# Loading k of batch 1 ahead of the weights, and moving batch 1's first attention steps ahead of batch 0's cosines

## The chip, the cores and the metric

The kernel runs on one core of a Trainium2 chip. The metric is the device time of one execution in microseconds (us). Lower is better. Each comparison was made on one chip, with the kernel before run in the same rounds. Nearly all executions fell in the normal ("fast") state, and only those are compared. The profiled execution gives the span, which is about 1.8 us shorter than the time.

## The reference

Two parts follow each other. An attention compresses k and v through 32 packed queries p, then attends from q to the result. A gated layer follows, with cos as the gate.

```python
# q, k, v: (8 batches, 8 heads, 576, 64), p: (8, 8, 32, 64), float32
p_packed = sm_attn(p, k, v)               # softmax(p k^T / 8) v
out      = sm_attn(q, p_packed, p_packed) # softmax(q p_packed^T / 8) p_packed
x = out.transpose(0, 2, 1, 3).reshape(8 * 576, 512)
h = x @ w_in                              # 512 -> 2048
y = (h * cos(h)) @ w_out                  # 2048 -> 512, written as float32 (4608, 512)
```

The kernel forms `PPW = p_packed @ w_in` for each batch, so that h of a batch comes straight from the normalised second softmax `a2n`.

## The kernel before

In the traces the instructions of each engine run in the order of the program (below, for one, SP holds a transpose back for 14 us behind another one). One stage per batch interleaves three things: the exps of batch s, then the 16 slices of its h (matmul on TensorE, cosine on ScalarE, multiply on VectorE), and "filler": the output matmuls of batch s-1, 16 for each of 4 or 5 chunks of rows. Three PSUM buffers (`psA`) serve everything but the output. Some names: `pe_T` transposes k or q on TensorE and `xbar` by DMA; `s1` is the scores and exps of p k^T, and `a1_pe` or `a1_xbar` transposes these exps (`a1`); `pp` forms the packed values and `ppw` one of the four pieces of PPW; `s2`, `sums2` and `normalise` are the second softmax; `dup_p` and `pack_p` prepare p; `warm` is matmuls on zeros whose result nobody reads; `gate` is a copy of one element, with which POOL waits for a tile. The parts that the change and the argument touch (cuts are marked `# ...`):

```python
def load(n, b):                       # k, v or q of a batch, float32 -> bf16, issued by POOL
    bf[n, b] = bf_pool.tile([TP, H, C * D], BF16, name=n + "bf", tag=n + "bf")   # one buffer each
    G.dma_start(out=bf[n, b], in_=...)

def xbar(n, b):                       # transpose by DMA, on the SP queue
    nc.sync.dma_start_transpose(out=xT[n, b], in_=bf[n, b]...)
def a1_xbar(b):                       # the same for a1, the exps of p k^T
    nc.sync.dma_start_transpose(out=a1T[b], in_=a1[b % 2]...)
def pp(b): ...                        # packed values: needs a1T and the permuted v

def out_gen(b):                       # one output matmul per next(); stores go out on the SP queue
    for c in range(n_chunks(b)):
        for fc in range(NFC): ...     # all of w_out for each chunk
        copy((V, ACT)[n_out[0] % 2], osb, ps)
        for a, z, rows in pieces_of(b, c):
            nc.sync.dma_start(out=rows, in_=osb[a:z, :])

# start: loads in the order k0 v0 q0, w_in (p in between), w_out, k1 v1 q1 k2 v2 q2
# ... attention of batch 0, then its h, then:
set_filler(0)
fill(4); pe_T("k", 1); fill(3); s1(1); permute_v(1, V); fill(8); a1_pe(1)   # ... 43 filler matmuls
# ... between the steps of batch 1's attention

def begin_loads(b):                   # POOL waits for the k transpose of b, then loads
    G.tensor_copy(out=gate, in_=xT["k", b][0:1, 0, 0:1])
    for n, i in (("v", b), ("q", b), ("k", b + 1)):
        load(n, i)

permute_v(2); xbar("q", 2); xbar("k", 3)          # ahead of the h of batch 1
slot(1, [...], [(8, lambda: begin_loads(3))])     # h of batch 1, loads hooked to slice 8

for s in range(2, B):
    # ...
    s2(s); fill(8)
    s1(s + 1)
    xbar("q", s + 1); xbar("k", s + 2); a1_xbar(s + 1)     # SP queue, in this order
    G.tensor_copy(out=gate, in_=a1T[s + 1][0:1, 0, 0, 0:1])  # later loads wait for a1T
    # ... sums, normalise, fill, loads of s + 2, then
    slot(s, [(5, lambda: pp(s + 1)), ...], [])
```

The softmax here doesn't subtract the row's maximum and nothing guards it: scores larger than these inputs give would overflow.

## Time and profile before

| | before |
|---|---|
| time, median of the first 3 runs | 266.17 us (263.6 to 266.24) |
| span of the profiled execution | 262.1 us |
| TensorE (PE) busy | 241.2 us, 92% |
| first cosine of batch 0 / last multiply of its h ends | 21.1 / 38.0 us |
| cosine table load ahead of the h of batch 1 / 2 / 3 / 7 | 56.4 / 82.9 / 112.9 / 224.5 us |

The last row is used as a set of markers: ScalarE loads a table when it changes between exps and cosines, and each stage has one such load ahead of its h. In the page, the first line below is the busy time of the engines. The other one is the TensorE clock that was granted, in tenths of full speed, for 40 equal slices of the span.

```profile
...
PE 241.2 (92%) x2003; PEld 132.1 (50%) x2037; DVE 158.7 (61%) x247; ACT 172.4 (66%) x276; POOL 53.8 (21%) x67
...
PEclk9997999999999999999999999999999999999999
...
```

Where TensorE idles is in the windows view of the kernel before (per window: its length, then busy time and count for each engine, granted clock, DMA share, GB/s):

```profile
...
0.00:20.00 20.00, 15.07 (x154) 8.04 (x157) 8.84 (x25) 8.79 (x16) 10.54 (x19) 1.00 1.06 175
20.00:40.00 20.00, 14.57 (x118) 8.62 (x119) 15.05 (x22) 14.03 (x20) 2.49 (x3) 0.91 1.26 206
40.00:80.00 40.00, 36.61 (x401) 20.57 (x406) 27.10 (x46) 26.72 (x48) 13.28 (x14) 1.00 1.09 177
80.00:240.00 160.00, 157.03 (x1241) 85.42 (x1262) 103.94 (x151) 120.67 (x191) 26.84 (x31) 1.00 0.70 130
...
```

Most of the idle time is in the first 80 us (13.8 us; another 4 are in the tail); from 80 to 240 us TensorE is busy 98% of the time. From 10 to 60 us the DMA engines are full as well (share above 1): k0, v0, q0, w_in, w_out, k1, v1, q1 and then batch 2's k, v and q land one after the other. The transposes of k1 on TensorE wait for that queue (timeline of the kernel before, TensorE):

```profile
...
39.01 1.15 PE L101 MATMUL psA<-ident,kbf 96*128 96x96 bf16 x23 [1.65 <-DMA kbf<-in_k_dram]
```

The bracket says that it was idle for 1.65 us and that the load of k1 ended it.

POOL passes its gate on k3 and issues the loads of v3, q3 and k4 from 68.1 us on (timeline of the kernel before, POOL), and TensorE waits for that a1 transpose only 0.3 us (waits view: us in total, times, longest):

```profile
...
68.01 0.18 POOL L410 COPY gate<-kT 1x1 bf16<-1x1 bf16 x1
...
68.90 0.77 POOL L83 DMA_DIRECT2D qbf<-in_q_dram  x1
...
```

```profile
...
PE psA L162 <- DMA a1T<-a: 0.3, 1, 0.3
...
```

### The profile page before, as it was taken

The page shows a single profiled execution, that of the slowest core. Times are in us where ns is not written, and L with a number is a line of the kernel's source. Part 1 is how long each engine was busy: PE and PEld are TensorE (multiplying, and loading weights), DVE is VectorE, ACT ScalarE, POOL GpSimd, SP SyncE. Part 2 cuts the span into 40 slices and gives each one's busy share as a digit, 9 for nine tenths or more (in the row PEclk, how much of TensorE's full clock was granted, in tenths as well). Part 3 has the DMA queues.
Part 4 walks back from the last instruction along what each step waited for, and adds up shares of the span by engine and source line. Part 5 has one row for each costly group of instructions (what it writes and reads, how often), then busy time and mean ns, then how long its engine had stood idle before and what let it go on. Part 6 is the DMA issues. An engine that isn't in the chain of part 4 may idle for free.

```text
span 262.1 us, 5030 instructions
## 1 busy us (share of the span) xinstructions
PE 241.2 (92%) x2003; PEld 132.1 (50%) x2037; DVE 158.7 (61%) x247; ACT 172.4 (66%) x276; POOL 53.8 (21%) x67
## 2 busy tenths in 40 slices
PE   8777769899989999999999999999999999999993
PEld 3433436555545555456545654564446544565452
DVE  2457876749854797268836684378735873678110
ACT  1377762496698657987797668866796568875000
POOL 8523002440431220504050303120040000000000
PEclk9997999999999999999999999999999999999999
DMA  6999999999399899499959992899193111121232
GB/s 94 203 226 207 206 204 197 200 193 199 48 203 203 184 175 177 89 188 174 220 107 189 165 225 64 149 186 173 52 165 106 40 43 40 42 50 31 80 83 80
DMA packets 62919, 37.09 MB, mean 142 GB/s; under 512 B 35520, under 2 KB 58304, under 8 KB 62896
## 3 DMA queue, kind: packets, MB, share of 16 engines
q0 software_dynamic: 23168, 18.81, 47.2%
q1 hardware_dynamic: 39568, 17.83, 31.3%
q8 instruction: 16, 0.26, 0.4%
q10 hardware_dynamic: 160, 0.13, 0.2%
q14 instruction: 7, 0.06, 0.1%
HBM read 37.22 MB, written 9.44 MB: 178 GB/s over the span
## 4 chain that ended last, share of the span: by engine, by line
PE 68%; DMA 14%; ACT 7%; DVE 5%; issue 2%; POOL 1%; SPq 0%; DVEq 0%; ACTq 0%; POOLq 0%
PE ot L270 40%; PE psA L220 18%; DMA kbf<-in_k_dram 7%; DMA w_in_bf<-in_moe_w_in_dram 5%; PE psA L181 3%; DVE gT L227 2%; PE psA L162 2%; DMA a1T<-a 1%; ACT L423 1%; PE psA L123 1%; ACT cosT L224 1%; PE ot L259 1%; ACT PPW L74 1%; PE psA L197 1%; PE psA L101 1%
## 5 line engine op out<-in xcount | busy, mean ns | idle before, releaser
L270 PE MATMUL ot<-w_out_bf,gT 128*128 128x512 bf16 x483 | 126.1, 380 | 2.1 <-issue 1.1
L227 DVE TENSOR_TENSOR gT<-psA,cosT 128x576 bf16<-128x576 f32 x128 | 95.0, 755 | 31.9 <-ACT cosT L224 29.2
L224 ACT ACTIVATE cosT<-psA 128x576 bf16<-128x576 f32 x128 | 83.2, 653 | 40.7 <-PE psA L220 38.4
L220 PE MATMUL psA<-a2n,PPW 128*128 128x288 bf16 x512 | 84.5, 289 | 6.5 <-DVE gT L227 3.0
L220 PEld LDWEIGHTS <-PPW 128*128 128x128 bf16 x512 | 50.4, 98 | 43.8 <-issue 12.8
L270 PEld LDWEIGHTS <-gT 128*128 128x128 bf16 x512 | 47.0, 98 | 42.8 <-issue 7.3
L231 POOL COPY joint<-gT 128x512 bf16<-128x512 bf16 x16 | 9.8, 614 | 109.2 <-DVE gT L227 109.2
L207 DVE SCALAR_TENSOR_TENSOR a2n<-a2u,r,lns 128x576 bf16<-128x576 bf16 x16 | 12.4, 815 | 17.8 <-ACT lns L205 17.8
L76 DVE COPY osb<-ot 128x512 f32<-128x512 f32 (+1 forms) x19 | 12.7, 671 | 15.1 <-PE ot L270 12.1
L76 DVE CAST PPW<-psA 128x1024 bf16<-128x1024 f32 x16 | 19.5, 1221 | 2.0 <-PE psA L181 1.9
L74 ACT COPY osb<-ot 128x512 f32<-128x512 f32 (+1 forms) x18 | 10.4, 575 | 15.2 <-PE ot L270 10.4
L74 ACT CAST PPW<-psA 128x1024 bf16<-128x1024 f32 x16 | 16.1, 1009 | 1.1 <-PE psA L181 1.1
L76 POOL COPY vp<-vbf 96x3072 bf16<-96x3072 bf16 x6 | 16.5, 2749 | 1.4 <-DMA vbf<-in_v_dram 1.4
L181 PE MATMUL psA<-w_in_bf,ppT 64*32 64x512 bf16 x256 | 13.3, 392 | 0.1
L189 ACT ACTIVATE a2u<-psA,rs 128x576 bf16<-128x576 f32 x16 | 11.0, 738 | 2.5 <-PE psA L123 2.4
L132 ACT ACTIVATE a<-psA 128x576 bf16<-128x576 f32 x16 | 10.3, 651 | 3.4 <-PE psA L123 3.4
L270 PE MATMUL ot<-w_out_bf,joint 128*128 128x512 bf16 x45 | 12.2, 380 | 0.2
L199 ACT ACTIVATE lns<-psA 128x576 f32<-128x576 f32 x16 | 10.5, 658 | 2.4 <-PE psA L197 2.4
L172 ACT CAST ppT<-psA 64x128 bf16<-64x128 f32 x16 | 4.2, 261 | 11.5 <-PE psA L101 6.4
L141 DVE RECIPROCAL r<-sums 128x2 f32<-128x2 f32 x8 | 1.3, 161 | 16.7 <-ACT a L132 16.7
L83 POOL DMA_DIRECT2D kbf<-in_k_dram x8 | 6.3, 789 | 21.0 <-PE psA L101 17.1
L224 ACT ACT_TABLE_LOAD x8 | 10.3, 1283 | 0.1
(54 smaller groups left out, 149.7 us busy)
## 6 DMA issues: line engine op xcount, KB each, us to landing
kbf<-in_k_dram POOLq DMA_DIRECT2D x8, 576.0 KB, 11.3
vbf<-in_v_dram POOLq DMA_DIRECT2D x8, 576.0 KB, 6.3
qbf<-in_q_dram POOLq DMA_DIRECT2D x8, 576.0 KB, 9.6
out_dram<-osb SPq DMA_DIRECT2D x24, 192.0 KB, 2.9
out_dram<-osb SPq DMA_DIRECT2D x22, 128.0 KB, 2.4
w_in_bf<-in_moe_w_in_dram POOLq DMA_DIRECT2D x4, 512.0 KB, 15.4
w_out_bf<-in_moe_w_out_dram POOLq DMA_DIRECT2D x4, 512.0 KB, 20.0
out_dram<-osb SPq DMA_DIRECT2D x26, 64.0 KB, 2.2
```

What stands on the lines that cost most here:

```text
L74: ACT.copy(out=out, in_=in_)
L76: eng.tensor_copy(out=out, in_=in_)
L132: ACT.activation(out=a1[b % 2][:, y, :, 0:TP].rearrange("p (e m) x -> p e m x", e=2), in_=ps[y][:, :, 0:HS].rearrange("p e (m x) -> p e m ...
L181: nc.tensor.matmul(ps[32 * x:32 * x + 32, y, :], ppT[b % 2][r, 2 * x + y, :], w_in_bf[r, x, n * 512:(n + 1) * 512], start=True, stop=True)
L189: ACT.activation(out=a2u[b][:, y].rearrange("p (e x) -> p e x", e=2), in_=ps[y][:, :, 0:HS], func=AF.Exp, scale=rs1[b][:, y:y + 1])
L199: ACT.activation(out=lns[b][:, y].rearrange("p (e x) -> p e x", e=2), in_=ps[:, :, 0:HS], func=AF.Ln)
L207: V.scalar_tensor_tensor(out=a2n[b][:, y], in0=a2u[b][:, y], scalar=r1[b][:, y:y + 1], in1=lns[b][:, y], op0=ALU.mult, op1=ALU.mult)
L220: nc.tensor.matmul(ps[:, e, 0:HS], PPW[b][:, y, fc * 128:(fc + 1) * 128], a2n[b][:, y, e * HS:(e + 1) * HS], start=(y == 0), stop=(y == 1))
L224: ACT.activation(out=csv, in_=ps[:, :, 0:HS], func=AF.Sin, bias=PI_HALF)
L227: V.tensor_tensor(out=gT[b][:, fc, :].rearrange("p (e x) -> p e x", e=2), in0=ps[:, :, 0:HS], in1=csv, op=ALU.mult)
L231: G.tensor_copy(out=joint[b // 2][:, fc - 7:fc + 1, j0:j0 + 64], in_=gT[b][:, fc - 7:fc + 1, 512:576])
L270: nc.tensor.matmul(ps, w, w_out_bf[:, fc, :], start=(fc == 0), stop=(fc == NFC - 1))
```

## The change

The intent: with k1 there early, the first half of batch 1's attention can use TensorE's idle time during batch 0's h. v1, q1 and k2 come ahead of w_out. The output of batch 0 goes by quarters of w_out, so that it can start before all of w_out is there. In the later stages some PPW pieces move to the exp phase. Cut to its core:

```diff
-    bf[n, b] = bf_pool.tile([TP, H, C * D], BF16, name=n + "bf", tag=n + "bf")
+    bf[n, b] = bf_pool.tile([TP, H, C * D], BF16, name=n + "bf", tag=n + "bf", bufs=2 if n == "k" else 1)
 # out_gen: chunks 0 and 1 of batch 0 together, by quarters of w_out
+    groups = [(0, 1), (2,), (3,)] if b == 0 else [(c,) for c in range(n_chunks(b))]
+    for grp in groups: ... for f0 in range(0, NFC, 4): for c in grp: for fc in range(f0, f0 + 4): ...
 # start: k0 v0 q0, then
-    w_in ... p ... w_out ... k1 v1 q1 k2 v2 q2
+    k1, w_in, p, (after s2(0)) v1 q1 k2 w_out, (after batch 0's h) v2 q2 k3
 # ahead of batch 0's h
+    pe_T("k", 1)
     normalise(0)
+    s1(1)
+    warm(4); ppw(0, 0); warm(4)
     for fc in range(NFC):
         h_mm(0, fc)()
+        # a1_pe(1) at 3, dup_p at 9, pack_p at 10, permute_v(1, V) at 11, pp(1) at 12, ppw(1, 0..1) at 15
 # between the h of batch 0 and of batch 1: 8 filler matmuls instead of 43
+    pe_T("q", 1); s2(1); ppw(1, 2, V); sums2(1, 0); sums2(1, 1); pe_T("k", 2); normalise(1)
+    s1(2); ppw(1, 3, V); a1_pe(2); recips(2); fill(8)
 # h of batch 1
-    permute_v(2); xbar("q", 2); xbar("k", 3)
-    slot(1, [... pp(2) at 7, pack_p at 9, PPW pieces at 1, 4, 11, 14], [(8, begin_loads(3))])
+    slot(1, [(6, pack_p), (8, permute_v(2, V)), (10, xbar("q", 2)), (11, pp(2)), (12, pw2(2)),
+             (13, xbar("k", 3)), (13, begin_loads(3))], 5)      # 5 filler matmuls are kept back
 # stages of batches 2 to 7
     s2(s)
+    ppw(s, 2, V)
     fill(8)
     s1(s + 1)
+    ppw(s, 3, V)
-    slot: pp(s+1) at 5, PPW pieces at 8, 10, 12, 14
+    slot: pp(s+1) at 5, pieces 0 and 1 at 9 (between 4 + 4 filler matmuls), 5 filler matmuls kept back
```

More of the change, by code (lines that the diff above doesn't have):

```diff
@@ L172, in pp, with ppw @@
             ACT.copy(out=t[z, :, y, :], in_=pv[r, :, y, :])
-    def ppw(b, n):
+    def ppw(b, n, eng=None):
         if b not in PPW:
@@ L182, in ppw @@
                                  w_in_bf[r, x, n * 512:(n + 1) * 512], start=True, stop=True)
-        copy((V, ACT)[n % 2], PPW[b][:, :, n * 512:(n + 1) * 512], ps)
+        copy(eng or (V, ACT)[n % 2], PPW[b][:, :, n * 512:(n + 1) * 512], ps)
     def s2(b):
@@ L265, in out_gen @@
     def out_gen(b):
-        for c in range(n_chunks(b)):
-            ps = O.tile([128, DM], FP32, name="ot", tag="ot")
-            for fc in range(NFC):
-                w = joint[b // 2][:, fc, :] if c == 4 else gT[b][:, fc, c * 128:(c + 1) * 128]
-                nc.tensor.matmul(ps, w, w_out_bf[:, fc, :], start=(fc == 0), stop=(fc == NFC - 1))
-                if fc < NFC - 1:
-                    yield
-            osb = o_pool.tile([128, DM], FP32, name="osb")
-            copy((V, ACT)[n_out[0] % 2], osb, ps)
-            n_out[0] += 1
-            for a, z, rows in pieces_of(b, c):
-                nc.sync.dma_start(out=rows, in_=osb[a:z, :])
-            yield
+        groups = [(0, 1), (2,), (3,)] if b == 0 else [(c,) for c in range(n_chunks(b))]
+        for grp in groups:
+            pss = {c: O.tile([128, DM], FP32, name="ot", tag="ot") for c in grp}
+            for f0 in range(0, NFC, 4):
+                for c in grp:
+                    for fc in range(f0, f0 + 4):
+                        w = joint[b // 2][:, fc, :] if c == 4 else gT[b][:, fc, c * 128:(c + 1) * 128]
+                        nc.tensor.matmul(pss[c], w, w_out_bf[:, fc, :],
+                                         start=(fc == 0), stop=(fc == NFC - 1))
+                        if fc == NFC - 1:
+                            osb = o_pool.tile([128, DM], FP32, name="osb")
+                            copy((V, ACT)[n_out[0] % 2], osb, pss[c])
+                            n_out[0] += 1
+                            for a, z, rows in pieces_of(b, c):
+                                nc.sync.dma_start(out=rows, in_=osb[a:z, :])
+                        yield
     filler = [None, 0]
@@ L307, in warm @@
             nc.tensor.matmul(wps, wz[:, 0:128], wz, start=True, stop=True)
-    nc.sync.dma_start(out=p_raw[:, 0:2, :], in_=p_rows[:, 0:2, :])
+    nc.sync.dma_start(out=p_raw[:, 0:4, :], in_=p_rows[:, 0:4, :])
     load("k", 0)
@@ L313 @@
     load("q", 0)
-    load_w_in(0)
-    load_w_in(1)
-    G.dma_start(out=p_raw[:, 2:, :], in_=p_rows[:, 2:, :])
-    load_w_in(2)
-    load_w_in(3)
-    for n in range(4):
-        load_w_out(n)
-    load("k", 1)
-    load("v", 1)
-    load("q", 1)
-    load("k", 2)
-    load("v", 2)
-    load("q", 2)
+    load("k", 1)
+    for n in range(4):
+        load_w_in(n)
+    G.dma_start(out=p_raw[:, 4:, :], in_=p_rows[:, 4:, :])
     wz = const.tile([128, 512], BF16, name="wz")
@@ L337 @@
     warm(7)
-    dup_p(0, 2)
-    pack_p(0, 1)
+    dup_p(0, 4)
+    pack_p(0, 2)
     warm(9)
@@ L349 @@
     s2(0)
-    ppw(0, 0)
+    load("v", 1)
+    load("q", 1)
+    load("k", 2)
+    for n in range(4):
+        load_w_out(n)
     sums2(0, 0)
     sums2(0, 1)
+    pe_T("k", 1)
     normalise(0)
-    warm(6)
-    dup_p(2, 16)
+    s1(1)
+    warm(4)
+    ppw(0, 0)
+    warm(4)
     for fc in range(NFC):
@@ L358, with slot, pw2 @@
         if fc in (1, 4, 7):
-            ppw(0, 1 + fc // 3)
-        if fc == 10:
-            pack_p(1, 3)
-    set_filler(0)
-    ACT.preload_act_table_set(EXP_SET)
-    fill(4)
-    pe_T("k", 1)
-    fill(3)
-    s1(1)
-    permute_v(1, V)
-    fill(8)
-    a1_pe(1)
-    recips(1)
-    fill(4)
-    pp(1)
-    pe_T("q", 1)
-    fill(3)
-    ppw(1, 0)
-    s2(1)
-    fill(4)
-    pe_T("k", 2)
-    ppw(1, 1)
-    fill(3)
-    s1(2)
-    fill(4)
-    sums2(1, 0)
-    fill(4)
-    sums2(1, 1)
-    normalise(1)
-    fill(6)
-    a1_pe(2)
-    recips(2)
+            ppw(0, 1 + fc // 3, ACT)
+        if fc == 3:
+            a1_pe(1)
+            recips(1)
+        if fc == 9:
+            dup_p(4, 16)
+        if fc == 10:
+            pack_p(2, 4)
+        if fc == 11:
+            permute_v(1, V)
+        if fc == 12:
+            pp(1)
+        if fc == 15:
+            ppw(1, 0)
+            ppw(1, 1)
+    load("v", 2)
+    load("q", 2)
     load("k", 3)
-    def slot(s, pieces, hooks):
-        left = filler[1]
+    def slot(s, hooks, keep=0):
+        left = filler[1] - keep
         for fc in range(NFC):
-            rest = h_mm(s, fc)
-            while pieces and pieces[0][0] == fc:
-                pieces.pop(0)[1]()
-            rest()
+            h_mm(s, fc)()
             while hooks and hooks[0][0] == fc:
                 hooks.pop(0)[1]()
-            done = left - filler[1]
+            done = left + keep - filler[1]
             fill((left * (fc + 1)) // NFC - done)
-    def pw(b, n):
-        return lambda: ppw(b, n)
+    def pw2(b):
+        fill(4)
+        ppw(b, 0)
+        ppw(b, 1)
+        fill(4)
     def begin_loads(b):
@@ L412, in begin_loads @@
             load(n, i)
-    permute_v(2)
-    xbar("q", 2)
-    xbar("k", 3)
-    slot(1, [(1, pw(1, 2)), (4, pw(1, 3)), (7, lambda: pp(2)), (9, lambda: pack_p(3, B)),
-             (11, pw(2, 0)), (14, pw(2, 1))], [(8, lambda: begin_loads(3))])
+    set_filler(0)
+    ACT.preload_act_table_set(EXP_SET)
+    pe_T("q", 1)
+    s2(1)
+    ppw(1, 2, V)
+    sums2(1, 0)
+    sums2(1, 1)
+    pe_T("k", 2)
+    normalise(1)
+    s1(2)
+    ppw(1, 3, V)
+    a1_pe(2)
+    recips(2)
+    fill(8)
+    slot(1, [(6, lambda: pack_p(4, B)), (8, lambda: permute_v(2, V)), (10, lambda: xbar("q", 2)),
+             (11, lambda: pp(2)), (12, lambda: pw2(2)), (13, lambda: xbar("k", 3)),
+             (13, lambda: begin_loads(3))], 5)
     for s in range(2, B):
         nxt = s + 1 < B
+        fill(1000)
         set_filler(s - 1)
@@ L435 @@
             G.tensor_copy(out=gate, in_=a1T[s + 1][0:1, 0, 0, 0:1])
+        else:
+            ppw(s, 3, V)
         fill(4)
@@ L444 @@
                 load(n, b)
-        pieces = [(1, pw(2, 2)), (4, pw(2, 3))] if s == 2 else []
-        if nxt:
-            pieces += [(5, lambda: pp(s + 1))] + [(8 + 2 * n, pw(s + 1, n)) for n in range(4)]
-        slot(s, pieces, [])
-        fill(1000)
+        slot(s, [(5, lambda: pp(s + 1)), (9, lambda: pw2(s + 1))] if nxt else [], 5)
     set_filler(B - 1)
```

## The prediction

> **What bounds the kernel now.** TensorE. The page gives it 241 of 262.1 us busy. In the timeline 13 back-to-back output matmuls (128x512) take 2.81 us, 216 ns each, which agrees with the Trainium skill ("TensorE: Matmul & The Clock Gate", Wait - 56ns): 215.7 ns warm. The windows view puts the idle TensorE time mostly at the start: 4.9 us in 0-20, 5.4 in 20-40, 3.4 in 40-80, only about 3 us in 80-240, and 4 in the tail. In the start the DMA engines are saturated and land in issue order at about 0.2 MB/us: k0 7.4, q0 13.4, the last w_out 36, k1 39.0. TensorE waits 1.65 us for k1, and the first 20 us also hold warming matmuls. h of batch 0 runs 20.0-37.2 us, batch 1's attention 39.0-56.7, filled with 43 output matmuls of batch 0; h of batch 1 (56.7-75.3) has only 21 left and runs 3 us longer than its matmuls need (16x0.49 + 21x0.216 + pieces = 15.6).
>
> **What the change does.** At 0.2 MB/us k1 lands near 16.3, w_in 19-27, v1 31, q1 34, k2 37, w_out 40-48: no load should stall TensorE. So the 1.65 us wait goes, and k1's transposes, scores, exps, a1 transposes, packed values and the first two PPW pieces move into the early phase. Against this:
> - First cosine: k1's three copies on VectorE (0.5 us each) delay a2n to 21.3, the PPW copy (1.2) follows, two exps (0.65 each) precede the table load: first cosine about 23.8 instead of 21.1.
> - h of batch 0: each slice holds one of three psA buffers for 0.65 matmul + 0.65 cosine + 0.76 multiply. Three PPW pieces, two a1 transposes, pack and pp take buffers of the same rotation, and VectorE gains a1T copies (1.0), permute (0.95) and ppT casts (0.6). Stepping through with the trace's durations, the loop takes 22 us instead of 17-18, ending near 45.3.
> - The chain q1 transposes, s2, exp, sums, Ln, Exp, a2n, then the exps of k2 and the table load now runs with only 8 filler matmuls at its end: h of batch 1 starts near 57, as before (56.7), but with 56 output matmuls left instead of 21 (7.6 us more) and two PPW pieces fewer (0.8).
> - h of batch 1 is then full: the 3 us of slack are recovered.
> Net there: 7.6 - 0.8 - 3 = about 4 us worse. Later stages: five held-back matmuls at each boundary and PPW pieces moved to the exp phase may recover about 1 us of the 3 idle. Loads of v3, q3, k4 start later (slice 13, not 8), so the a1T transpose of batch 3, behind the others on the SP queue, may be 0-1 us late.
>
> **Prediction.** About 1 us gained late, 3 lost early, shaded for the chance that the early loop overlaps better than I count: 267.8 us against 266.17; range 262.0 to 272.5. Faster by over 2% 0.07, within 2% 0.72, slower by over 2% 0.21.
>
> **What would show it.** Right: no wait of transposes for k1; first cosine near 23.8; last multiply of batch 0's h near 45; TensorE under 70% busy in 23-57; first h matmul of batch 1 at 55-58; its slot about 21 us long at over 97% busy; late stages 0.1-0.3 us shorter each. Wrong: batch 1's h starting before 53, or a stall on w_out or v1.
>
> **What would make it wrong.** The early loop faster than the three-buffer count (then a gain of 1-2%); the clock throttling again in the sparse early phase, or a late a1T (then slower still).

## More of the kernel before

For later use, the SP queue's own part of the timeline of the kernel before, around the stage of batch 2 (for SP the duration is that of the issue, not of the transfer):

```profile
...
60.20 2.96 SPq L92 DMA_TRANSPOSE kT<-kbf  x1
63.24 13.64 SPq L277 DMA_DIRECT2D out_dram<-osb  x4
78.33 3.81 SPq L92 DMA_TRANSPOSE qT<-qbf  x1
82.31 2.97 SPq L92 DMA_TRANSPOSE kT<-kbf  x1
85.33 1.56 SPq L146 DMA_TRANSPOSE a1T<-a  x1
...
```

The transpose of k3 goes out at 60.2 us, ahead of the output stores, and that of a1 of batch 3 at 85.3 us.

## The result, and the profile after

| | before | after |
|---|---|---|
| time, median | 265.84 us (263.6 to 266.24, 4 runs) | 278.93 us (278.41 to 281.0, 4 runs) |
| ratio of the fast runs | 1 | 1.0525 (95%: 1.0445 to 1.0605) |
| span of the profiled execution | 262.1 us | 277.1 us |
| first cosine / last multiply of batch 0's h ends | 21.1 / 38.0 us | 26.4 / 48.1 us |
| table load ahead of h of batch 1 | 56.4 | 56.7 (+0.3) |
| ... of batch 2 | 82.9 | 90.4 (+7.5) |
| ... of batch 3 | 112.9 | 129.0 (+16.0) |
| ... of batch 7 | 224.5 | 239.5 (+15.0) |

A ratio is the mean time of one kernel's fast runs over that of the other's fast runs of the same rounds, so it is not quite the ratio of the medians. The change costs 5%. The markers place the loss: 7 us between the h of batch 1 and of batch 2, where the prediction had 4, another 8.5 us in the stage of batch 2, where it had at most 1, and then 1 us regained, as predicted.

The same lines of the page of the changed kernel:

```profile
...
PE 244.4 (88%) x2009; PEld 136.8 (49%) x2039; DVE 165.6 (60%) x254; ACT 166.6 (60%) x270; POOL 50.7 (18%) x66
...
PEclk9977995999999995999999999999999999999999
...
```

PE's busy time rose by 3 us for almost the same matmuls (two more warming ones). The Trainium skill ("Trainium Kernel Development and Optimization", Performance Expectations) calls matmul busy time a bad metric, because matmuls are pipelined; here it counts matmuls at half clock as busy, and this trace agrees that it does not measure the work. The granted clock shows new dips. By windows of 0.5 us of the same trace it was half in 17.3 to 24.2 us, 41.2 to 48.0 us and 102.7 to 109.5 us, 6.8 us each time; in the kernel before only in 22.9 to 26.3 us.

The largest waits of TensorE in the changed kernel (waits view: us in total, times, longest):

```profile
...
PE psA L162 <- DMA a1T<-a: 8.0, 1, 8.0
PE psA L220 <- DVE gT L227: 3.6, 8, 0.7
...
```

The 1.65 us wait for k1 is gone, as intended. In its place the packed-value matmuls of batch 3 (L162) wait 8.0 us for a1T, once; next come eight short waits for psA buffers, 3.6 us together (3.0 in the kernel before). The SP and POOL parts of the timeline of the changed kernel say why:

```profile
...
71.42 3.22 SPq L92 DMA_TRANSPOSE qT<-qbf  x1
78.47 0.84 SPq L280 DMA_DIRECT2D out_dram<-osb  x2
79.42 3.62 SPq L92 DMA_TRANSPOSE kT<-kbf  x1
...
94.48 3.63 SPq L92 DMA_TRANSPOSE qT<-qbf  x1
98.29 2.86 SPq L92 DMA_TRANSPOSE kT<-kbf  x1
101.20 1.67 SPq L146 DMA_TRANSPOSE a1T<-a  x1
...
```

```profile
...
84.64 0.18 POOL L395 COPY gate<-kT 1x1 bf16<-1x1 bf16 x1 [14.07 <-DMA kT<-kbf]
85.18 0.77 POOL L83 DMA_DIRECT2D vbf<-in_v_dram  x1 [0.36 <-issue]
85.94 0.77 POOL L83 DMA_DIRECT2D qbf<-in_q_dram  x1
86.70 0.77 POOL L83 DMA_DIRECT2D kbf<-in_k_dram  x1
...
```

Read from the bottom of the chain: the a1 transpose goes out at 101.2 us instead of 85.3, though the exps that it reads were done at 86.7. It stands behind the q3 transpose, which could not go before 94.5 us, because q3 was not there (SP waited 10.2 us for it, below): POOL issued the loads of v3, q3 and k4 from 85.2 us on, after it had waited 14.07 us for the k3 transpose (the gate). That transpose stands at 79.4 us behind an output store (78.47). In the kernel before, it went at 60.2 us. The wait of SP (waits view), and the chain of waits of the changed kernel, which runs over these very steps:

```profile
...
SPq L92 <- DMA qbf<-in_q_dram: 10.2, 1, 10.2
...
```

```profile
...
97.31 0.80 SPq L92
...
98.29 2.86 SPq L92
...
101.20 3.93 DMA a1T<-a
...
105.27 1.44 PE psA L162 x24
...
```

Last, the stretch between the h of batch 0 and of batch 1 (windows view of the changed kernel):

```profile
...
23.00:57.00 34.00, 24.26 (x268) 14.08 (x267) 23.88 (x38) 22.20 (x37) 5.48 (x8) 0.88 1.10 178
57.00:80.00 23.00, 21.75 (x170) 12.86 (x171) 16.05 (x26) 12.67 (x20) 0.62 (x1) 1.00 0.42 81
...
```

TensorE is busy 71% of 23 to 57 us (predicted: under 70), at 0.88 of its clock.

### The profile page after: what moved, and what is told of

It reads as the page before. It is cut to its first block, busy times and chain, and to the rows that moved or that the text cites. A ratio compares the mean times of both kernels' runs of the same rounds, so it can differ in the third digit from the quotient of the medians.

```text
span 277.1 us, 5039 instructions
## 1 busy us (share of the span) xinstructions
PE 244.4 (88%) x2009; PEld 136.8 (49%) x2039; DVE 165.6 (60%) x254; ACT 166.6 (60%) x270; POOL 50.7 (18%) x66
## 4 chain that ended last, share of the span: by engine, by line
PE 72%; ACT 9%; DVE 8%; DMA 5%; issue 2%; SPq 1%; POOL 1%; DVEq 0%; ACTq 0%; POOLq 0%
PE ot L273 40%; PE psA L220 21%; DVE gT L227 4%; DMA qbf<-in_q_dram 4%; ACT cosT L224 3%; PE psA L162 2%; ACT a2u L189 2%; PE psA L181 2%; PE psA L197 2%; DMA a1T<-a 1%; ACT L421 1%; PE psA L123 1%; SPq L92 1%; DVE PPW L76 1%; PE ot L259 1%
## 5 line engine op out<-in xcount | busy, mean ns | idle before, releaser
L227 DVE TENSOR_TENSOR gT<-psA,cosT 128x576 bf16<-128x576 f32 x128 | 94.0, 754 | 42.9 <-ACT cosT L224 42.0
L224 ACT ACTIVATE cosT<-psA 128x576 bf16<-128x576 f32 x128 | 81.1, 652 | 38.9 <-PE psA L220 37.6
L220 PE MATMUL psA<-a2n,PPW 128*128 128x288 bf16 x512 | 83.0, 291 | 4.7 <-DVE gT L227 3.6
L273 PEld LDWEIGHTS <-gT 128*128 128x128 bf16 x512 | 48.5, 98 | 44.0 <-issue 6.2
L76 DVE CAST PPW<-psA 128x1024 bf16<-128x1024 f32 x22 | 26.9, 1221 | 14.3 <-PE psA L181 14.3
L207 DVE SCALAR_TENSOR_TENSOR a2n<-a2u,r,lns 128x576 bf16<-128x576 bf16 x16 | 12.4, 814 | 10.2 <-ACT lns L205 10.2
L162 PE MATMUL psA<-a1T,vp 96*128 96x64 bf16 x192 | 8.1, 205 | 10.6 <-DMA a1T<-a 8.0
L76 POOL COPY vp<-vbf 96x3072 bf16<-96x3072 bf16 x5 | 13.8, 2751 | 3.5 <-DMA vbf<-in_v_dram 3.5
L162 PEld LDWEIGHTS <-vp 96*128 96x128 bf16 x192 | 7.6, 106 | 11.5 <-issue 9.0
L74 ACT CAST PPW<-psA 128x1024 bf16<-128x1024 f32 x10 | 10.1, 1012 | 4.2 <-PE psA L181 4.1
L310 PE MATMUL wps<-wz 128*128 128x512 bf16 x25 | 9.6, 539 | 1.7 <-DVE wz L323 1.2
```

The source lines that it names most:

```text
L74: ACT.copy(out=out, in_=in_)
L76: eng.tensor_copy(out=out, in_=in_)
L162: nc.tensor.matmul(ps[:, 0, hp * 64:(hp + 1) * 64], vp[b][:, c, hp * 128:(hp + 1) * 128], a1T[b][0:TP, :, j, 32 * hp:32 * hp + 32], start= ...
L207: V.scalar_tensor_tensor(out=a2n[b][:, y], in0=a2u[b][:, y], scalar=r1[b][:, y:y + 1], in1=lns[b][:, y], op0=ALU.mult, op1=ALU.mult)
L220: nc.tensor.matmul(ps[:, e, 0:HS], PPW[b][:, y, fc * 128:(fc + 1) * 128], a2n[b][:, y, e * HS:(e + 1) * HS], start=(y == 0), stop=(y == 1))
L224: ACT.activation(out=csv, in_=ps[:, :, 0:HS], func=AF.Sin, bias=PI_HALF)
```

## The experiments

There are two theories for the loss after batch 1. **Loads:** v3, q3 and k4 are loaded too late, and the a1 transpose of batch 3 stands behind them. **Clock and early phase:** the sparse early phase and its half clock push everything back, and the late transpose is only a symptom. A third question is what the late part of the change (stages of batches 2 to 7) is worth.

### The a1 transpose first on the SP queue

```diff
+            if s == 2:
+                a1_xbar(s + 1)
             xbar("q", s + 1)
             if s + 2 < B:
                 xbar("k", s + 2)
-            a1_xbar(s + 1)
+            if s != 2:
+                a1_xbar(s + 1)
```

> The changed kernel with one edit: in the stage of batch 2 the a1 transpose of batch 3 stands ahead of the q3 and k4 transposes on the SP queue; the loads stay late. Theory (the a1 transpose is ready at 87 us but queues behind the q3 transpose, which waits 10.2 us for the late q3 load): the wait of the packed-value matmuls for a1T falls from 8.0 us to under 1, the clock dip at 104-111 us goes, time 268 to 271 us instead of 278.9. Rival (the late v3 load itself holds the packed values, through its permute): the wait stays above 4 us and the time above 274 us.

Measured: 277.1 us, ratio 1.0438 (1.0361 to 1.0515; one run of 279.36 us was slow and is left out). The wait fell only to 4.9 us. Both numbers lie on the rival's side (over 4 us, over 274), but its reason is not what the trace shows: v3 was permuted by 95.9 us, and the packed values waited for a1T until 103.3. The transpose did go out at 88.0 us, but it landed 15.2 us later. In the changed kernel it takes 3.9. The issues of a1_first from 86 to 104 us (KB each, us from issue to landing):

```profile
...
vbf<-in_v_dram POOLq DMA_DIRECT2D x1, 576.0 KB, 6.6
qbf<-in_q_dram POOLq DMA_DIRECT2D x1, 576.0 KB, 11.9
kbf<-in_k_dram POOLq DMA_DIRECT2D x1, 576.0 KB, 15.0
a1T<-a SPq DMA_TRANSPOSE x1, 15.2
...
```

So the order of the SP queue is one cause of the wait (the intervals of the two ratios overlap, so a gain in time is not shown), and taking it away alone uncovers another: the transpose now shares the DMA engines with three loads in flight. The Trainium skill ("DMA: Bandwidth & Descriptors", Queues, rings and completion order) says that each DMA engine takes turns between the queues that have work, packet by packet; a transpose slowed by loads of another queue agrees with it. The next run tests that.

### Only v3 in flight

As above, but q3 and k4 are loaded and transposed after the a1 transpose:

```diff
 def begin_loads(b):
-    for n, i in (("v", b), ("q", b), ("k", b + 1)):
-        load(n, i)
+    load("v", b)
 # stage of batch 2: a1_xbar(3) alone on the SP queue; after the gate on a1T
+    load("q", 3); load("k", 4)
 # and after fill(13)
+    xbar("q", 3); xbar("k", 4)
```

> As a1_first, but only v3 is loaded ahead of the a1 transpose of batch 3; q3 and k4 are loaded, and transposed, after it. In a1_first the a1 transpose went out at 88.0 us, unblocked, and still took 15.2 us to land instead of 3.9, while the loads of v3, q3 and k4 (1.77 MB) filled the DMA engines. Theory now (the transpose shares the DMA engines with the loads in flight and is slowed by them): with one load in flight instead of three it lands within 5 to 9 us of its issue, the wait of the packed-value matmuls falls from 4.9 us to under 1, time 269 to 273 us. Rival (something else delays that transpose, such as the q and k transposes that were ahead of it): it still takes over 12 us, time 275 or more.

Measured: the a1 transpose of batch 3 landed 6.5 us after its issue, and no wait for it was left in the stage of batch 2 (table loads of h at 90.0 and 119.4 us, 29.4 us apart instead of 38.6). The mechanism held. The time did not: 277.82 us, ratio 1.0459 (1.0395 to 1.0523). The same wait, now 6.0 us, had moved one stage on, to the packed values of batch 4, because q4's load waited 14.78 us for the late q3 transpose (waits view, 120 to 150 us, and POOL's timeline of this run):

```profile
...
PE psA L162 <- DMA a1T<-a: 6.0, 1, 6.0
...
```

```profile
...
111.43 0.77 POOL L83 DMA_DIRECT2D qbf<-in_q_dram  x1 [14.78 <-DMA qT<-qbf]
...
```

So here the lateness was handed on to the next stage.

### All hooks early

```diff
-    slot(1, [(6, pack_p(4, B)), (8, permute_v(2, V)), (10, xbar("q", 2)), (11, pp(2)),
-             (12, pw2(2)), (13, xbar("k", 3)), (13, begin_loads(3))], 5)
+    slot(1, [(2, permute_v(2, V)), (3, xbar("q", 2)), (3, xbar("k", 3)), (4, begin_loads(3)),
+             (6, pack_p(4, B)), (11, pp(2)), (12, pw2(2))], 5)
```

> The changed kernel with the hooks of batch 1's slot moved: permute of v2, q2 and k3 transposes and the loads of v3, q3, k4 at slices 2 to 4 instead of 8 to 13. Theory: q3 lands before its transpose is reached, so the a1 transpose is on time with the SP order unchanged; same gain as with the order changed, 268 to 271 us. If the lateness of the loads is not the origin of the wait, the time stays near 279.

Measured: 268.36 us, ratio 1.0118 (1.0052 to 1.0184). As the loads theory expected: TensorE no longer waits for the DMA transpose of a1, and in the profile the clock does not dip after 44 us. That profile is the fastest of the four runs, 266.22 us at a mean clock of 0.994; the other three took 268.14 to 268.75 us at 0.974 to 0.981.

### The late hooks alone, in the kernel before

```diff
-    xbar("k", 3)
-    slot(1, [...], [(8, begin_loads(3))])
+    slot(1, [...], [(13, xbar("k", 3)), (13, begin_loads(3))])
```

> The kernel before with one thing of the change: in batch 1's slot the k3 transpose stands at slice 13 instead of ahead of the slot, and the loads of v3, q3, k4 at slice 13 instead of 8. Theory (the late loads, which wait for that transpose, are enough to make the a1 transpose of batch 3 late, whatever the early phase does): a wait of 4 to 9 us of the packed-value matmuls for a1T, time 269 to 275 us, ratio 1.015 to 1.04. Rival (it takes the changed early phase and its fuller slot as well): no such wait, ratio within 0.995 to 1.005.

Measured: 265.1, 265.6 and 267.6 us, ratio 1.0032 (0.9969 to 1.0096), so the rival's side: the late slice alone does not do it. The profiled execution was useless: it took 485.3 us (see the last section). So it was run once more for a profile.

> The same kernel as before_late_hooks once more, for a usable profile: the first one fell in an execution of 485 us in which every matmul took twice as long. Its timed runs (265.1 to 267.6 us) already say that the late hooks alone cost little. Theory now (with them the late loads still leave the a1 transpose in time, because in the kernel before k3's transpose goes out and the slot ends with more room): loads of v3, q3, k4 issued before 80 us, a wait of the packed-value matmuls for a1T under 2 us. Rival (the wait is there, 4 us or more, and something else in that kernel pays for it): a wait of 4 us or more with the time still under 268 us.

Measured: one run, 266.94 us; two waits for a1T of 2.1 us together, the longest 1.1, so just over the 2 us of the theory. Here the k3 transpose went out on SP at 65.3 us and the loads at 71.2 to 72.7 us, early enough, from the same slice. That put the question: what places the k3 transpose on SP, if not its slice?

### One line moved

In the changed kernel, the k3 transpose at slice 3 of batch 1's slot instead of 13. The load hooks stay at 13.

```diff
-    slot(1, [(6, pack_p(4, B)), ..., (12, pw2(2)), (13, xbar("k", 3)), (13, begin_loads(3))], 5)
+    slot(1, [(3, xbar("k", 3)), (6, pack_p(4, B)), ..., (12, pw2(2)), (13, begin_loads(3))], 5)
```

> The changed kernel with one line moved: the k3 transpose stands on the SP queue at slice 3 of batch 1's slot, ahead of the output stores of that slot, instead of at slice 13, behind them. The loads of v3, q3, k4 keep their place in the program. Theory (on its own queue each engine runs in order, so it is not the slice number that made the loads late but that they wait for a transpose that stands behind an output store of the second last chunk; in the changed kernel the store goes out at 78.5 us, the transpose at 79.4, the loads at 85.2): loads out at 71 to 76 us, wait for a1T under 1.5 us, time 267 to 271 us as with all hooks moved (loads_early, 268.4). Rival (the slice of the load hooks itself is what counts): loads still after 80 us, time over 274 us.

Measured: 268.01 us, ratio 1.0126 (1.0085 to 1.0167), the same as with all hooks early. SP and POOL in that run:

```profile
...
59.60 3.12 SPq L92 DMA_TRANSPOSE kT<-kbf  x1
67.51 2.06 SPq L280 DMA_DIRECT2D out_dram<-osb  x4
...
84.90 3.75 SPq L92 DMA_TRANSPOSE qT<-qbf  x1
...
91.83 1.59 SPq L146 DMA_TRANSPOSE a1T<-a  x1
...
```

```profile
...
68.77 0.18 POOL L395 COPY gate<-kT 1x1 bf16<-1x1 bf16 x1
71.04 0.77 POOL L83 DMA_DIRECT2D vbf<-in_v_dram  x1 [2.10 <-DVE vp L76]
78.23 0.77 POOL L83 DMA_DIRECT2D qbf<-in_q_dram  x1 [6.42 <-DMA qT<-qbf]
78.99 0.77 POOL L83 DMA_DIRECT2D kbf<-in_k_dram  x1
...
```

And its waits view:

```profile
...
PE psA L162 <- DMA a1T<-a: 1.0, 1, 1.0
...
```

The wait for a1T fell to 1.0 us. v3 went out at 71.0 us as expected, q3 and k4 at 78.2 and 79.0 us, later than expected (they still wait for the q2 transpose), and that was early enough. So one line placed a loss of 4% (1.0525 over 1.0126, each beside the kernel before). The k3 transpose waits on SP for the output store that stands ahead of it in the program. In the fuller slot of the changed kernel that store comes late (78.5 us); with the same slice in the kernel before, the store ahead of it went at 64.4 us. The load hook at slice 13 by itself does not hold POOL back: POOL passed the gate at 68.8 us, right after the copy for slice 7, and the loads then waited for what the program does with their buffers: v3 for the permute of v2, q3 for the q2 transpose.

### The late part alone

The kernel before with the change's stages of batches 2 to 7.

> The kernel before with only the late part of the change (stages of batches 2 to 7: two PPW pieces in the exp phase, two in the middle of the slot, five output matmuls held back to the stage boundary). Theory: small gain, 0.5 to 2 us below before (the later stages in the changed kernel regain 1.0 us between 129 and 240 us). Rival: the late part costs time and hides a part of the loss; then over 266.5.

Measured: 263.08 us, ratio 0.9918 (0.9852 to 0.9985). The late part is worth 0.8%. If the two parts add, the early part with the loads in time is worth 1.0118 (all hooks early, the same sitting) over 0.9918, a loss of 2.0%; with k3_early (1.0126) it is 2.1%. The next runs look for its cause.

### Warming matmuls, and filler

First the warming matmuls, beside the reordered SP queue:

```diff
+    warm(3)
     sums2(0, 0)
 # in the h of batch 0
+        if fc == 9: dup_p(4, 16); warm(8)
+        if fc == 12: warm(8); pp(1)
```

> As a1_first, with warming matmuls put where TensorE waits in the early phase: 3 before the first sums of batch 0, 8 before the pack of P and 8 before the packed values of batch 1. They stand ahead of matmuls that wait anyway. Theory (the clock is granted at half in 17-24 and 41-48 us because TensorE had idled before; this costs 1 to 3 us): granted clock 1.0 in 40-50 us, h of batch 1 starts 1 to 3 us earlier than in a1_first, time 1 to 3 us lower. Rival (VectorE and the three psA buffers set the pace there, the clock does not matter): same time within 0.7 us although the clock is up, or no change of the clock.

Measured: 273.76 us, ratio 1.031 against 1.0438, so about 1.3% better. The marker of batch 1 came 1.1 us earlier (54.95 against 56.07), and part of the rest was a shorter wait for a1T later, 4.0 us at the longest against 4.9 (one run of 276.08 us was slow and is left out). The clock was full up to 44 us but half from about 47 us on, so the expected cure came only in part. It was tried again without the late loads:

> As loads_early, with the warming matmuls of a1_first_warm (3 before the first sums, 8 before the pack of P, 8 before the packed values of batch 1). Theory (half clock in the early phase costs 1 to 3 us of the 3 us by which loads_early is behind the kernel before): 264.5 to 267.5 us, ratio to before 0.998 to 1.008. Rival (the clock there is worth nothing): ratio 1.010 to 1.016 as in loads_early.

Measured: 268.54 us, ratio 1.0142 (1.011 to 1.0175) against 1.0118: nothing, as the rival had it. But here too the clock was half in part of the early phase (second table below), so this run does not say what the clock is worth, and the gain in the run before is not shown to be the clock's. Then filler was added, 26 more output matmuls spread over the chain between the h of batch 0 and of batch 1:

```diff
+    fill(4)
     pe_T("q", 1)
+    fill(4)
     s2(1)
     ppw(1, 2, V)
+    fill(3)
     sums2(1, 0)
+    fill(2)
     sums2(1, 1)
+    fill(3)
     pe_T("k", 2)
+    fill(4)
     normalise(1)
     s1(2)
+    fill(3)
     ppw(1, 3, V)
+    fill(3)
     a1_pe(2)
     recips(2)
     fill(8)
```

> As loads_early_warm, with 26 more output matmuls of batch 0 spread over the attention of batch 1 (in the changed kernel only 8, all at its end). Theory (the unfilled chain between the h of batch 0 and of batch 1, where TensorE is 70% busy, is the remaining early loss): 2 to 4 us less than loads_early_warm, ratio to before 0.985 to 0.998. Rival (the filled matmuls only lengthen that chain, as TensorE is in order): same as loads_early_warm within 1 us.

Measured: 262.12 us, ratio 0.9909 (0.9877 to 0.9941). Filler brought 2.3% in the same sitting, and the changed kernel now beats the kernel before. It beats it only by what the late part alone brings (0.9918): the repaired early part neither costs nor gains anything that these runs can tell. The windows view shows both effects; first loads_early_warm, then loads_early_warm_fill:

```profile
...
44.00:48.00 4.00, 2.90 (x54) 2.05 (x51) 3.65 (x6) 2.29 (x2) 1.75 (x3) 0.71 0.76 116
48.00:52.00 4.00, 3.73 (x41) 2.31 (x41) 1.78 (x2) 3.49 (x6) 1.14 (x2) 0.50 1.26 187
...
```

```profile
...
44.00:48.00 4.00, 3.74 (x71) 2.16 (x63) 3.52 (x6) 2.38 (x3) 2.36 (x4) 1.00 0.79 118
48.00:52.00 4.00, 4.00 (x48) 2.50 (x40) 2.30 (x4) 3.70 (x6) 0.53 (x1) 1.00 1.22 181
...
```

With filler the clock stays at 1.00, and the idle time at 44 to 48 us falls from 1.10 to 0.26 us. The busy times of the first run are those of half-speed matmuls. Finally, filler without the warming matmuls:

> As loads_early_warm_fill without the warming matmuls. The spread output matmuls brought 2.3% beside the warming ones; this tells the two apart. Theory (the filling did it, by using TensorE's idle time and by keeping its clock up; the warming matmuls are worth nothing): ratio to before within 0.4% of the 0.991 of loads_early_warm_fill. Rival (both are needed, the clock falls in the early loop without the warming): ratio 0.997 or more, mean clock below 0.985.

Measured: 264.93 us, ratio 0.9991 (0.9941 to 1.0041), mean granted clock 0.968 to 0.987 in its six runs against 0.996 to 1.0 with warming. The theory of this run fell: warming matmuls are worth nothing without filler, and 0.8% with it; filler without them is worth 1.3% (0.9991 over 1.0118; different sittings, each beside the kernel before). The clocks fit this reading: warming keeps the clock up through the sparse loop, filler in the chain after it, and if either is missing it falls.

### The load order in the kernel before

The kernel before with the late part, and with k1, v1 and q1 loaded after w_in and ahead of w_out; the early order of work is untouched. First with the output of batch 0 by quarters of w_out:

```diff
-    for n in range(4):
-        load_w_out(n)
     load("k", 1)
     load("v", 1)
     load("q", 1)
+    for n in range(4):
+        load_w_out(n)
 # plus out_gen by quarters, plus the late part
```

> The kernel before with three things: the late part (as late_only, 0.992 of before), k1, v1 and q1 loaded after w_in and ahead of w_out, and the output of batch 0 by quarters of w_out, so that the first output matmuls need only its first quarter. The early sequence of work stays as in before. Theory (before waits 1.65 us for k1 at 39 us, and it is the load order alone that was worth changing there): 1 to 3 us below late_only, ratio 0.98 to 0.988. Rival (the fillers now wait for w_out, which lands 9 us later): ratio 0.992 or more.

> As order_quarters_late, but with the output of batch 0 by whole chunks as in before. Theory (quarters matter once w_out is loaded last: the first chunk needs the last quarter of w_out after 16 matmuls instead of after 28, and it lands near 45 us): a wait of output matmuls for w_out of 1 to 3 us at 42 to 45 us, ratio 0.990 to 0.996 against 0.986. Rival (the load order alone is worth it, quarters nothing): ratio within 0.3% of 0.986.

Measured: with quarters 260.91 us, ratio 0.9864 (0.9831 to 0.9896), correct: the fastest version here. Without quarters 264.23 us, ratio 0.9978 (0.9934 to 1.0022), no better than the late part alone (0.9918, in another sitting; the intervals overlap). It came out a little above its expectation on both counts (0.990 to 0.996, a wait of 1 to 3 us). It has a wait for w_out, 3.3 us, that the quarters take away. With quarters the ratio is clear of that without them; against the late part alone the intervals overlap, so what the load order and the quarters add to it is not certain. Order_late, then order_quarters_late, waits of 20 to 60 us:

```profile
...
PE ot L270 <- DMA w_out_bf<-in_moe_w_out_dram: 3.3, 2, 1.7
...
```

```profile
...
PE ot L273 <- DMA w_out_bf<-in_moe_w_out_dram: 0.5, 1, 0.5
...
```

## Why the prediction was wrong

- **The bound, and the early phase.** The reasoning held, the sizes were a little small. It said that k1 would not be waited for (right), that batch 0's h would stretch to 22 us and end near 45 us (it took from 25.7 to 48.1 us), and that batch 1's h would start near 57 us with 35 more output matmuls left (58.9 us). The first cosine came at 26.4 us instead of 23.8. The clock was at half from 17.3 to 24.2 us; in the profile of k3_early, with the same instructions there and the full clock, it came at 24.4. The prediction named the clock as a risk and gave it no time. The slot of batch 1 was 95% busy and not over 97%, and its 16 slices took 21.3 us as predicted.
- **The net of the early phase.** "Net there: [...] about 4 us worse" was too small. With the loads in time (k3_early), the marker of batch 2 is 5.8 us behind the kernel before (88.6 against 82.9).
- **The late part.** "may recover about 1 us" fits the 1.0 us that the markers of the changed kernel regain from batch 3 to batch 7. Alone the late part brought 0.8%, 2.2 us, with an interval (0.15 to 1.5%) that does not rule out 1 us.
- **The step that failed.** "the a1T transpose of batch 3, behind the others on the SP queue, may be 0-1 us late." It named the mechanism and mis-sized it. The wait was 8.0 us, and the clock fell to half for 6.8 us with it: the stage of batch 2 took 38.6 us between the markers against 30.1 before and 29.6 in k3_early. The cause of the wrong size: the prediction placed the loads in time by the slice of their hook ("slice 13, not 8"). The runs show that their time is set by the k3 transpose, which stands on SP behind an output store (79.4 us), by the gate on it (84.6), and by the q3 load that the q3 transpose waits for (10.2 us).
- **The total.** k3_early is the changed kernel without that step: 268.0 us, against 267.8 predicted. So the range missed by this one term, 4% of the time. That the two agree so well is partly luck: the early phase cost more than predicted, and the number given was shaded and not the plain sum. The chance given to slower by over 2% was 0.21.
- **What stays open.** How much of the early loss is the clock and how much is idle time was not separated to better than the 0.8% that warming brings beside filler. The four runs of loads_early, one kernel, give another hint: 266.2 us at a mean clock of 0.994 and 268.1 to 268.8 us at 0.974 to 0.981, so some 2 us. Why the clock fell at 17.3 us in this profile and not in that of k3_early, with the same instructions there, is not shown either; the runs of one kernel differ in it.

## What to carry to other kernels

On a queue that runs in order, an instruction's time is set by what stands ahead of it on that queue and by what it waits for itself, and the loop slice at which the program names it says little of either: before moving a hook, list that queue and ask when its predecessor can go. Loads that other transfers or gates depend on need to be followed through the whole chain (gate, load, transpose, transpose behind it), because lateness can be handed to the next stage, as in the run with only v3 in flight. A chain of small dependent steps like the one here gains from independent filler matmuls in its gaps; here they came with less idle time and a fuller clock, and the two were not told apart.

## What the Trainium skill lacked or had wrong

- "TensorE: Matmul & The Clock Gate" (HAM oscillation) gives as the abstract rule that TensorE idle gaps of more than about 3.4 us lose the clock. In the changed kernel it fell to half at 41.2 us after gaps of at most 2.0 us, and at 17.3 us after gaps of at most 0.7 us (from 8 us on) between small matmuls. The page's next section (A second HAM failure mode: psum-queue depth-cycling) does name frequent short idle times as a second way to lose it, but gives no length for them. It stayed down 6.8 us each time, two of the page's windows of 3.413 us, and 3.4 us in the kernel before, one of them; in that the page agrees.
- The same page lets activity release the clock. One of some 100 executions here took 485.3 us: 13 output matmuls in a row took 6.27 us against 2.97 in the kernel before, DVE and ACT were busy about as usual (163 and 176 us), and the page of that run has no line of granted clock at all (the 1.0 in its result therefore rests on no record). That resembles a clock that was never released, which is argued and not shown; the matmuls started 443 ns apart (median), and at the half clock of the other traces 426. The page mentions a clock seen stuck at a quarter for more than 50 us, not for a whole execution.
- "DMA: Bandwidth & Descriptors" says that a transpose next to ordinary DMAs needs nothing, which is about correct data. It has no number for the cost: the a1 transpose landed 3.9 us after its issue with no load in flight, 6.5 us beside one load of 576 KB and 15.2 us beside three.
- "ScalarE: Activation LUTs" (What ACT_TABLE_LOAD costs) puts a table switch at about 2.66 us, 1.28 us of load and 1.38 us of drain. The load took 1.28 us here too, but no drain is seen around it: in the changed kernel a copy ends at 82.85 us, the load runs from 82.86 to 84.14 us, and the next exp starts at 84.16 us.
